# Ordered, gated loads and 256-token pieces in layer 1 of the first batch of a windowed-attention and MLP kernel

## The chip, the cores and the metric
The kernel runs on one NeuronCore of a Trainium2 chip. The metric is the device time of one execution in microseconds (us); lower is better.

## What is computed
Attention over four batches of 768 tokens, 8 heads of 64, in which a query sees the first 4 tokens and the 128 tokens up to its own, and then a two-layer MLP with a squared ReLU on the concatenated heads:

```
scores = q @ k.T / 8          # (4, 8, 768, 768), fp32 inputs
keep   = (key < 4) | (0 <= query - key < 128)
a      = softmax(where(keep, scores, -1e9))
x      = (a @ v) as (3072, 512)
out    = square(relu(x @ w_in)) @ w_out     # w_in (512, 2048), w_out (2048, 512)
```

## The kernel before
All work is written as small operations (`op`, L47) with the engines that may run them, what they come after, and which buffers they take. `Plan.run` (L50) walks through them once, while the program is built, and fixes for each engine an order of instructions; on the chip each engine runs its own list in order and waits on semaphores. So a planned time moves an instruction in a list, and only the list reaches the chip.

A batch goes through these steps. q and k are loaded in fp32 into `qr` and v into `vf` (`load_qk`, L267, `load_v`, L283, both on SP's queue), two heads to a load. `regroup` casts q and k to bf16 (`qs`), PE transposes them into PSUM (`pt`, L342), `unload` copies them to `qkT_sb`. `cast` brings v to bf16 (`v_sb`). `sink_scores` (`pk`) and `scores` (`ps`, L421) multiply, ScalarE takes the exponentials (`es`, `expm`, L435), `domask` multiplies a mask in on VectorE or cuts triangles on GpSimd, `values` (`po`, L470) multiplies with v, `norm` divides by the row sum, `bridge` (`px`, L498) transposes again, and `bridge_copy` writes `xT`. These run in steps s of 256 tokens; s = 0 and 1 are the first 512 tokens, s = 2 the rest. Batch 0 is loaded in two groups, `GROUPS[0]`: 512 tokens and 256; other batches in one.

Layer 1 (`layer1`, L510) multiplies xT with `w_in_sb` into `pm` (L521), ScalarE applies the ReLU (`r`, three buffers), VectorE squares into `gT_sb`. Its pieces are 2 blocks of 128 features by 512 tokens, then 4 blocks by 256 tokens for the last 256. Layer 2 (`layer2`, L536) multiplies `gT_sb` with `w_out_sb` into `py` (L554); the result is copied to `osb` (two buffers) and stored by SP. All PSUM tiles share four banks of 4 KB a partition. Attention of batch b+1 is planned among the two layers of batch b.

The weights come by GpSimd's queue with a cast to bf16: w_in in two halves of 1024 features (`load_w_in`), w_out in four pieces of 512 rows (`load_w_out`). Half 0 of w_in is made to wait for a v load of batch 0; half 1 and w_out wait for nothing of the kind. A DMA on SP also waits, in the built program, for the eighth DMA before it on that queue.

Of the kernel before, what the change touches and what calls it, by code (L numbers as in the profile page):

```python
# [16 lines left out]
LATENCY = 0.2  # L17
# [11 lines left out]
class Op:  # L29
    def __init__(self, key, engines, run, after, takes, reads, dma):  # L30
        self.key, self.engines, self.run = key, engines, run
        self.after, self.takes, self.reads, self.dma = list(after), list(takes), list(reads), dma
        self.end = None


class Plan:
# [4 lines left out]

    def __init__(self, capacity):
        self.ops, self.capacity = [], dict(capacity)

    def op(self, key, engines, run, after=(), takes=(), reads=(), dma=0.0):
        o = Op(key, engines, run, after, takes, reads, dma)
        self.ops.append(o)  # L47
        return o

    def run(self):  # L50
# [4 lines left out]
        blockers = {id(o): len(o.after) for o in waiting}  # L55
        users = {}
        for o in waiting:
            for a in o.after:
                users.setdefault(id(a), []).append(o)
# [4 lines left out]
        while left:  # L64
            best = None
            for o in ready:
# [10 lines left out]
                if not ok:  # L77
                    continue
                pick = None
# [21 lines left out]
            o.end = end  # L101
# [5 lines left out]
            for u in users.get(id(o), ()):  # L107
                blockers[id(u)] -= 1
                if not blockers[id(u)]:
                    u.at = max(a.end for a in u.after) + LATENCY  # L110
# [5 lines left out]
def kernel(  # L116
# [28 lines left out]
    sizes = dict(bank=4, qr=10, qs=6, vf=4, expm=8, r=3, osb=2)  # L145
# [16 lines left out]
    vs_in = consts.tile([32, B, D + 1], BF16)  # L162
# [28 lines left out]
    def build_ident(e):  # L191
        nc.vector.memset(ident, 1.0)
        nc.gpsimd.affine_select(out=ident, in_=ident, compare_op=ALU.is_equal, fill=0.0,
                                base=0, pattern=[[-1, 128]], channel_multiplier=1)

# [7 lines left out]
    def build_masks(e):  # L203
        nc.vector.memset(tri, 1.0)
        for i in range(2):
            triangles(tri[:, i:i + 1, :], i, 1)
        for h2 in range(2):
# [5 lines left out]
    def build_sink_constants(e):  # L213
        nc.vector.memset(head_rows, 1.0)
        nc.vector.memset(vs_in[:, :, D:D + 1], 1.0)
        for i in range(2):
            nc.vector.memset(kblk[i], 0.0)
            nc.vector.memset(vs_sb[i], 0.0)
            nc.vector.memset(v_sb[i][:, :, :, D:D + 1], 1.0)
# [7 lines left out]

    c_ident = op(-9, {"pool": 0.5}, build_ident)
    c_masks = op(-0.95, {"pool": 1.5}, build_masks)
    c_sinks = op(-0.94, {"pool": 1.0}, build_sink_constants)  # L230
    c_vs = op(-0.93, {"pool": 0.3},
              lambda e: nc.gpsimd.dma_start(out=vs_in[:, :, 0:D],
                                            in_=v[:, :, 0:NSINK, :].rearrange("b h s d -> (h s) b d"))
              if False else [nc.gpsimd.dma_start(out=vs_in[:, b, 0:D], in_=v[b, :, 0:NSINK, :])
                             for b in range(B)],
              after=[c_sinks], dma=0.2)
# [5 lines left out]
    def load_w_in(half, behind):  # L242
        def run(e):
            c = slice(half * (DFF // 2), (half + 1) * (DFF // 2))
            d = nc.gpsimd.dma_start(out=w_in_sb[:, :, c],
                                    in_=moe_w_in[:, c].rearrange("(a p) f -> p a f", p=128))
            if behind is not None:
                after_dma(d, loaded[behind])
            loaded["w_in", half] = d
        w_in_op[half] = op(-0.9 + 0.01 * half, {"pool": 0.6}, run, dma=5.5,  # L250
                           after=[ops[behind]] if behind is not None else ())

    def load_w_out(i):
        def run(e):
            nc.gpsimd.dma_start(
                out=w_out_sb[:, 4 * i:4 * i + 4, :],
                in_=moe_w_out[512 * i:512 * i + 512, :].rearrange("(f p) m -> p f m", p=128))
        w_out_op[i] = op(-0.8 + 0.01 * i, {"pool": 0.6}, run, dma=3.1)
# [7 lines left out]
    GROUPS[0] = [(0, 4), (512, 2)]  # L266

    def load_qk(key, b, m, ti, g, behind=None):
        t0, n = GROUPS[b][g]
        sl = qr_slot[b, m, ti, g] = Slot("qr", 1)  # L270

        def run(e):
            t = qr_t[b, m, ti, g] = work["qr"].tile([128, 2, n * D], FP32, name="qr", tag="qr")
            d = nc.sync.dma_start(  # L274
                out=t,
                in_=(q, k)[ti][b, 2 * m:2 * m + 2, t0:t0 + 128 * n, :].rearrange(
                    "h (p t) d -> p h (t d)", t=n))
            if behind is not None:
                after_dma(d, loaded[behind])
            loaded["qk", b, m, ti, g] = d  # L280
        ops["qk", b, m, ti, g] = op(key, {"sp": 0.1}, run, takes=[sl], dma=16 * (0.012 + n * 256 / 27200.0),
                                    after=[ops[behind]] if behind is not None else ())

    def load_v(key, b, m, g, behind=None):
        t0, n = GROUPS[b][g]
        sl = vf_slot[b, m, g] = Slot("vf", 1)

        def run(e):
            t = vf_t[b, m, g] = work["vf"].tile([128, 2, n, D], FP32, name="vf", tag="vf")
            for h2 in range(2):  # L290
# [380 lines left out]
```

## Time and profile before

| | us |
|---|---|
| median of 3 runs | 265.12 (264.98 to 265.88) |
| the profiled execution | 264.97 |
| its span, first to last instruction | 263.2 |
| PE busy in the span | 223.0 (85%) |
| ScalarE, VectorE, GpSimd busy | 136.2, 118.9, 33.1 |
| first matmul of layer 1, batch 0 | 42.98 |
| first matmul of layer 1, batch 1 | 109.83 |

The rows further down come from this one execution. A matmul's end is modelled and successive matmuls overlap, so a cost per matmul is read from a run of them in the chain of work (a run's time over its count), not from the mean duration. Idle time in brackets names what ended it.

### The profile page before, as it was taken

The numbers are of one execution on the slowest core, as the hardware profiler recorded it, in microseconds if no ns is written. First come the engines' busy times: TensorE is split into PE (matmuls) and PEld (weight loads), VectorE is DVE, ScalarE is ACT, GpSimd is POOL, SyncE is SP. The second block draws the span as 40 slices with busy tenths as digits, with TensorE's granted clock in tenths as the row PEclk, the third lists the DMA queues.
The fourth block names the chain that finished last, engine by engine and source line by source line (L and its number), as shares of the span: only waits on it lengthen the run. The fifth ranks groups of instructions, "written<-read, shape, count | busy, mean of one in ns | idle before, by whom it ended". The sixth has DMA issues, their size and how long they took to land.

```text
span 263.2 us, 4650 instructions
## 1 busy us (share of the span) xinstructions
PE 223.0 (85%) x1913; PEld 133.1 (51%) x1940; DVE 118.9 (45%) x273; ACT 136.2 (52%) x156; POOL 33.1 (13%) x49
## 2 busy tenths in 40 slices
PE   0711068999999988999999999999999999999983
PEld 0510055457565446745755456457654564484431
DVE  6520384689421048955654246457551544331010
ACT  1733014688954098876972455568525455561020
POOL 5710301106000003820000013000000110000000
PEclk9965559999999997999999999999999999999998
DMA  6999998899999952000000120200000312000041
GB/s 197 244 195 196 251 234 234 281 217 307 325 238 349 226 190 82 2 0 2 1 2 0 48 114 4 80 0 2 0 4 0 121 40 82 0 0 2 0 176 63
DMA packets 42885, 29.68 MB, mean 113 GB/s; under 512 B 26480, under 2 KB 38768, under 8 KB 42864
## 3 DMA queue, kind: packets, MB, share of 16 engines
q1 hardware_dynamic: 39376, 25.17, 34.0%
q0 software_dynamic: 3488, 4.21, 9.2%
q8 instruction: 15, 0.25, 0.4%
q14 instruction: 6, 0.05, 0.1%
HBM read 27.30 MB, written 6.29 MB: 128 GB/s over the span
## 4 chain that ended last, share of the span: by engine, by line
PE 73%; SPq 9%; DVE 6%; ACT 6%; DMA 3%; issue 2%; DVEq 0%; ACTq 0%
PE py L554 31%; PE pm L521 29%; SPq L291 7%; PE po L470 5%; DMA qr<-in_q_dram 3%; PE ps L421 3%; ACT r L529 2%; PE pt L342 2%; PE px L498 2%; ACT expm L435 2%; SPq L274 2%; DVE xn_sb L484 1%; PE pk L391 1%; DVE expm L444 1%; DVE gT_sb L534 1%
## 5 line engine op out<-in xcount | busy, mean ns | idle before, releaser
L554 PE MATMUL py<-w_out_sb,gT_sb 128*128 128x512 bf16 x367 | 86.5, 379 | 2.5 <-DVE osb L179 0.8
L521 PE MATMUL pm<-xT,w_in_sb 128*128 128x256 bf16 (+1 forms) x504 | 86.1, 325 | 1.4 <-ACT xT L177 0.9
L521 PEld LDWEIGHTS <-w_in_sb 128*128 128x128 bf16 x512 | 49.6, 98 | 33.8 <-issue 1.7
L529 ACT ACTIVATE r<-pm 128x1024 bf16<-128x1024 f32 x48 | 49.1, 1025 | 29.1 <-PE pm L521 24.7
L554 PEld LDWEIGHTS <-gT_sb 128*128 128x128 bf16 x384 | 35.9, 98 | 41.9 <-issue 3.8
L435 ACT ACTIVATE expm<-ps 128x1024 bf16<-128x1024 f32 (+1 forms) x48 | 42.9, 953 | 19.6 <-PE ps L421 19.3
L534 DVE TENSOR_TENSOR gT_sb<-r 128x1024 bf16<-128x1024 bf16 x48 | 33.2, 691 | 43.6 <-ACT r L529 43.6
L444 DVE TENSOR_TENSOR expm<-expm,mask 128x1024 bf16<-128x1024 bf16 (+1 forms) x41 | 26.4, 657 | 32.8 <-ACT expm L435 32.1
L342 PE MATMUL pt<-ident,qs 128*128 128x128 bf16 x192 | 15.2, 236 | 20.0 <-POOL qs L181 12.5
L198 POOL TENSOR_SCALAR_AFFINE_SELECT expm<-expm 128x512 bf16<-128x512 bf16 x14 | 8.6, 635 | 133.1 <-ACT expm L435 133.1
L177 ACT ACTIVATE osb<-py 128x1024 f32<-128x1024 f32 (+1 forms) x9 | 8.4, 952 | 31.3 <-PE py L554 13.6
L342 PEld LDWEIGHTS <-qs 128*128 128x128 bf16 x192 | 12.9, 105 | 22.7 <-POOL qs L181 12.9
L421 PE MATMUL ps<-qkT_sb 64*128 64x128 bf16 (+1 forms) x256 | 16.0, 252 | 8.2 <-DVE qkT_sb L179 5.6
L470 PEld LDWEIGHTS <-expm 128*128 128x128 bf16 x352 | 18.6, 103 | 4.6 <-issue 1.5
L470 PE MATMUL po<-v,expm 128*128 128x65 bf16 x352 | 19.8, 202 | 1.0 <-ACT expm L435 0.6
L177 ACT ACTIVATE qkT_sb<-pt 128x768 bf16<-128x768 bf16 (+1 forms) x18 | 13.4, 768 | 9.8 <-PE pt L342 5.5
L484 DVE TENSOR_TENSOR xn_sb<-po,rc 128x256 bf16<-128x256 f32 x48 | 18.1, 419 | 0.0
L179 DVE COPY qkT_sb<-pt 128x768 bf16<-128x768 bf16 (+2 forms) x22 | 15.2, 710 | 6.3 <-PE pt L342 4.0
L421 PEld LDWEIGHTS <-qkT_sb 64*128 64x128 bf16 x256 | 9.3, 99 | 15.9 <-issue 13.8
L177 ACT ACTIVATE xT<-px 128x1024 bf16<-128x1024 bf16 x8 | 8.2, 1024 | 17.0 <-PE px L498 16.9
L179 DVE COPY osb<-py 128x1024 f32<-128x1024 f32 (+2 forms) x5 | 4.8, 956 | 23.9 <-PE py L554 19.3
L470 PE MATMUL po<-vs,es 128*128 128x65 bf16 x128 | 14.3, 199 | 0.0
(38 smaller groups left out, 104.9 us busy)
## 6 DMA issues: line engine op xcount, KB each, us to landing
out_dram<-osb SPq DMA_DIRECT2D x11, 512.0 KB, 2.9
qr<-in_k_dram SPq DMA_DIRECT2D x12, 384.0 KB, 6.7
qr<-in_q_dram SPq DMA_DIRECT2D x12, 384.0 KB, 6.6
vf<-in_v_dram SPq DMA_DIRECT2D x24, 192.0 KB, 4.4
w_in_sb<-in_moe_w_in_dram POOLq DMA_DIRECT2D x2, 1024.0 KB, 12.0
w_out_sb<-in_moe_w_out_dram POOLq DMA_DIRECT2D x4, 512.0 KB, 13.6
qr<-in_k_dram SPq DMA_DIRECT2D x4, 256.0 KB, 4.5
qr<-in_q_dram SPq DMA_DIRECT2D x4, 256.0 KB, 4.9
```

What stands on the lines that cost most here:

```text
L177: nc.scalar.activation(out=dst, in_=src, func=AF.Copy)
L179: nc.vector.tensor_copy(out=dst, in_=src)
L342: nc.tensor.matmul(pt[:, ti, 128 * t:128 * t + 128], lhsT=qs[:, t, :, :], rhs=ident, is_transpose=True, start=(t == 0), stop=(t == n - 1))
L421: nc.tensor.matmul(ps[:, h2, o:o + w], lhsT=qkT_sb[r, m, 1, 128 * c:128 * c + 128], rhs=qkT_sb[r, m, 0, 128 * qb:128 * qb + w], start=(i = ...
L435: nc.scalar.activation(out=x[:, :, o:512], in_=bank_t["s", b, s, m][:, :, o:512], func=AF.Exp, scale=scale)
L444: nc.vector.tensor_mul(x[:, :, o:512], x[:, :, o:512], mk[:, :, o:512])
L470: nc.tensor.matmul(pv[:, i, h2, :], lhsT=lhsT, rhs=rhs, start=(n_ == 0), stop=(n_ == len(mms) - 1))
L484: nc.vector.tensor_tensor(out=xn_sb[:, 2 * s + i, 128 * m0:128 * m0 + 256].rearrange("p (j h d) -> p j h d", j=2, d=D), in0=pv[:, i, :, :, ...
L521: nc.tensor.matmul(pm[:, i, :], lhsT=w_in_sb[:, kb, 128 * fb:128 * fb + 128], rhs=xT[:, kb, c0:c0 + cw], start=(kb == 0), stop=(kb == NKB ...
L529: nc.scalar.activation(out=r, in_=bank_t.pop(tag), func=AF.Relu)
L534: (nc.vector if e == "dve" else nc.gpsimd).tensor_mul(gT_sb[:, fbs[0]:fbs[0] + n, c0:c0 + cw], r, r)
L554: nc.tensor.matmul(pm[:, i, :], lhsT=gT_sb[:, fb, 128 * t:128 * t + 128], rhs=w_out_sb[:, fb, :], start=(fb == 0), stop=(fb == NFB - 1))
```

## The change
- All loads of a queue are written in one stated order (`dma_op`), and a chain keeps the plan from reordering them. SP: q, k of batch 0's first 512 tokens; v of these; the four sink loads; q, k, v of its last 256; then batches 1, 2 and 3.
- Loads are larger: q and k go four heads at a time (the first two pairs by two heads), v by tiles of 128 tokens and all 8 heads.
- Gates: w_in half 0 behind the second v tile; batch 0's last 256 tokens behind w_in half 0; w_out behind the first v tile of these; batch 1 behind the third piece of w_out.
- `qr` has 5 buffers of four heads instead of 10 of two, `vf` 3 of 256 tokens. `cast` goes by steps of 256 tokens.
- Batch 0's layer 1 runs its first 512 tokens as 4 blocks by 256 tokens, in the order (half 0, s 0), (half 0, s 1), (half 1, s 0), (half 1, s 1) by their keys; what PE's list makes of it has the first piece of half 1 in third place.
- Constants: all fills go to VectorE first; masks are copied behind them; the sink rows (`vs_in`) become fp32 and move from GpSimd's queue to SP's.
- The plan counts the eight DMAs that a queue may have outstanding.

```diff
-    sizes = dict(bank=4, qr=10, qs=6, vf=4, expm=8, r=3, osb=2)
+    sizes = dict(bank=4, qr=5, qs=6, vf=3, expm=8, r=3, osb=2)
...
+                if o.dma:
+                    past = landed.get(next(iter(o.engines)), ())
+                    if len(past) >= 8:
+                        t = max(t, past[-8])
...
+    def dma_op(queue, name, run, us, behind=None, takes=()):
+
+        def go(e):
+            ds = run(e)
             if behind is not None:
...
+                for d in ds:
+                    after_dma(d, loaded[behind])
+            loaded[name] = ds[-1]
+        o = op(-5, {queue: 0.5 if queue == "sp" else 0.85}, go, dma=us, takes=takes,
+               follow=[chained[queue]] if queue in chained else (),
+               after=[ops[behind]] if behind is not None else ())
+        ops[name] = chained[queue] = o
+        return o
...
+    def load_v(b, s, behind=None):
+
+        sl = vf_slot[b, s] = Slot("vf", 1)
+        for i in range(2):
+            t = 2 * s + i
...
+                return [nc.sync.dma_start(
+                    out=vf_t[b, s][:, i], in_=v[b, :, 128 * t:128 * t + 128, :].rearrange("h p d -> p h d"))]
...
-    for m in range(NP):
+    for m0, nm in ((0, 1), (1, 1), (2, 2)):
         for ti in (1, 0):
-            load_qk(-3 + 0.01 * m, 0, m, ti, first)
-    for m in range(NP):
-        load_v(-2 + 0.01 * m, 0, m, first)
-    load_w_in(0, ("v", 0, 2, first))
-    load_w_in(1, None)
...
+            load_qk(0, m0, nm, ti, first)
+    for s in range(2):
+        load_v(0, s)
+    c_vs = dma_op("sp", "vs_in", lambda e: [
+        nc.sync.dma_start(out=vs_in[:, b, 0:D], in_=v[b, :, 0:NSINK, :]) for b in range(B)], 0.2)
...
+    load_w_in(0, 5.7, ("v", 0, 1))
+    load_w_in(1, 8.7)
+    for m0 in (0, 2):
         for ti in (1, 0):
...
+            load_qk(0, m0, 2, ti, rest, behind=("w_in", 0) if m0 == 0 and ti == 1 else None)
+    load_v(0, 2)
     for i in range(4):
-        load_w_out(i)
+        load_w_out(i, ("v", 0, 4) if i == 0 else None)
+    BEHIND = {1: ("w_out", 2), 2: None, 3: None}
...
-        for i, fb in enumerate(range(0, NFB, 2)):
-            layer1(b, b + 0.333 * i / 8, (fb, fb + 1), 0, 512, (0, 1))
+        if b == 0:
+            for half in range(2):
+                for s in range(2):
+                    for i in range(2):
+                        fb = 8 * half + 4 * i
+                        layer1(b, 0.167 * half + 0.083 * s + 0.042 * i, range(fb, fb + 4), 256 * s, 256, (s,))
+        else:
+            for i, fb in enumerate(range(0, NFB, 2)):
+                layer1(b, b + 0.333 * i / 8, (fb, fb + 1), 0, 512, (0, 1))
```

SP's queue at the start, before (two heads to a load; `128x2x256` is 128 partitions of 2 heads by 256 numbers, four tokens each):

```order
L274 DMA qr<-in_k_dram 128x2x256
L274 DMA qr<-in_q_dram 128x2x256
L291 DMA vf<-in_v_dram 128x4x64 x8
L274 DMA qr<-in_k_dram 128x2x128
L274 DMA qr<-in_q_dram 128x2x128
```

The same queue after, whole from its third load to batch 1's first v:

```order
L301 DMA qr<-in_k_dram 128x2x256
L301 DMA qr<-in_q_dram 128x2x256
L301 DMA qr<-in_k_dram 128x4x256
L301 DMA qr<-in_q_dram 128x4x256
L318 DMA vf<-in_v_dram 128x8x64 x4
L625 DMA vs_in<-in_v_dram 32x1x64 x4
L301 DMA qr<-in_k_dram 128x4x128
L301 DMA qr<-in_q_dram 128x4x128
L301 DMA qr<-in_k_dram 128x4x128
L301 DMA qr<-in_q_dram 128x4x128
L318 DMA vf<-in_v_dram 128x8x64 x2
L301 DMA qr<-in_k_dram 128x4x384
```

Eight loads of q and k became six, eight of v four; before, batch 1's first loads stood among batch 0's last ones, now they stand behind all of these.

GpSimd's queue at the start, before:

```order
L221 AFFINE_SELECT head_rows<-head_rows 32x8
L224 AFFINE_SELECT head_rows<-head_rows 32x8
L245 DMA w_in_sb<-in_moe_w_in_dram 128x4x1024
L234 DMA vs_in<-in_v_dram 32x1x64 x4
L255 DMA w_out_sb<-in_moe_w_out_dram 128x4x512 x4
L181 CAST v_99<-vf 128x2x4x64
L245 DMA w_in_sb<-in_moe_w_in_dram 128x4x1024
```

And after:

```order
L233 AFFINE_SELECT head_rows<-head_rows 32x8
L236 AFFINE_SELECT head_rows<-head_rows 32x8
L270 DMA w_in_sb<-in_moe_w_in_dram 128x4x1024 x2
L201 AFFINE_SELECT expm<-expm 128x4x128 x4
L189 CAST qs<-qr 128x256 x5
L277 DMA w_out_sb<-in_moe_w_out_dram 128x4x512 x4
L201 AFFINE_SELECT expm<-expm 128x4x128 x2
```

Both halves of w_in now stand ahead of w_out, and behind the waiting w_in and w_out issues stand triangle cuts and casts of batch 0.

ScalarE around the first layer-1 results of batch 1 (`r`; `v_100` is here batch 3's v), before:

```order
L435 ACTIVATE expm<-ps 128x1024 x2
L177 ACTIVATE xT_103<-px 128x4x256
L177 ACTIVATE qkT_sb<-pt 128x768 x4
L177 ACTIVATE v_100<-vf 128x12x64
L529 ACTIVATE r<-pm 128x1024 x7
```

And after:

```order
L457 ACTIVATE expm<-ps 128x1024 x8
L185 ACTIVATE xT_103<-px 128x4x256
L185 ACTIVATE qkT_sb<-pt 128x768 x3
L185 ACTIVATE v_100<-vf 128x2x8x64
L551 ACTIVATE r<-pm 128x1024 x2
```

The cast of batch 3's v stands ahead of batch 1's layer-1 results in both.

## Rows read from the trace of the kernel before

**Rows 1.** The page's 40 slices of 6.58 us, tenths: PE, granted clock, DMA.
```profile
PE   0711068999999988999999999999999999999983
...
PEclk9965559999999997999999999999999999999998
DMA  6999998899999952000000120200000312000041
```

**Rows 2.** Busy us of engines by stage, then granted clock, DMA share, GB/s.
```profile
0.00:42.98 42.98, 13.49 (x172) 10.62 (x173) 20.73 (x66) 14.02 (x19) 12.60 (x23) 0.72 1.07 227
42.98:109.83 66.85, 62.42 (x598) 39.02 (x605) 34.28 (x78) 45.66 (x54) 11.15 (x13) 0.97 0.84 225
109.83:263.20 153.37, 147.03 (x1145) 83.49 (x1162) 63.89 (x131) 76.50 (x83) 9.32 (x14) 0.99 0.08 32
```

**Rows 3.** Timeline of the start: start, us, engine, line, operation, [idle before <-releaser].
```profile
4.33 0.93 POOL L245 DMA_DIRECT2D w_in_sb<-in_moe_w_in_dram  x1
...
4.87 19.14 SPq L291 DMA_DIRECT2D vf<-in_v_dram  x8
...
8.93 2.33 POOL L255 DMA_DIRECT2D w_out_sb<-in_moe_w_out_dram  x3
...
30.39 0.43 DVE L179 CAST v<-vf 128x512 bf16<-128x512 f32 x1 [10.34 <-DMA vf<-in_v_dram]
...
30.83 0.74 POOL L245 DMA_DIRECT2D w_in_sb<-in_moe_w_in_dram  x1 [5.39 <-DMA vf<-in_v_dram]
...
40.86 2.07 ACT L177 ACTIVATE xT<-px 128x1024 bf16<-128x1024 bf16 x2 [3.06 <-PE px L498]
...
42.98 2.32 PE L521 MATMUL pm<-xT,w_in_sb 128*128 128x512 bf16 x9 [0.89 <-ACT xT L177]
```

**Rows 4.** The tile w_in_sb: from issue to landing of its two loads.
```profile
DMA to landing us min/median/max: 11.7/12.0/12.4
```

**Rows 5.** Four stretches of 4 us, columns as in rows 2; GB/s stands last.
```profile
0.00:4.00 4.00, 0.00 (x0) 0.00 (x0) 2.23 (x15) 1.28 (x1) 1.07 (x8) 1.00 0.49 147
4.00:8.00 4.00, 1.70 (x16) 1.63 (x16) 3.00 (x10) 0.60 (x1) 3.93 (x6) 1.00 0.94 283
...
64.00:68.00 4.00, 3.21 (x32) 2.04 (x31) 3.96 (x11) 2.84 (x5) 1.11 (x1) 1.00 1.03 366
...
88.00:92.00 4.00, 4.00 (x20) 1.80 (x19) 0.00 (x0) 0.00 (x0) 0.00 (x0) 1.00 1.16 209
```

**Rows 6.** The page's DMA queue of the weights: packets, MB, share of 16 engines.
```profile
q0 software_dynamic: 3488, 4.21, 9.2%
```

**Rows 7.** The tile vf: from issue to landing of the v loads.
```profile
DMA to landing us min/median/max: 1.9/5.5/16.7
```

**Rows 8.** Groups by shape: the long exponentials; busy us, mean ns, idle before.
```profile
L435 ACT ACTIVATE expm<-ps 128x1024 bf16<-128x1024 f32 x32 | 31.1, 1023 | 15.5 <-PE ps L421 15.3
```

**Rows 9.** The chain of work in order of time: start, us, engine, tile, count.
```profile
37.07 2.58 PE po L470 x48
...
75.90 1.75 PE pm L521 x16
77.64 0.86 PE py L554 x4
...
155.99 0.55 PE ps L421 x12
...
157.51 0.74 PE po L470 x24
...
159.11 0.45 PE px L498 x8
159.56 0.67 PE pt L342 x12
```

**Rows 10.** Timeline of SP's queue, and of ScalarE later: batch 3's v.
```profile
81.62 9.27 SPq L291 DMA_DIRECT2D vf<-in_v_dram  x8
...
111.82 0.84 ACT L177 ACTIVATE v<-vf 128x768 bf16<-128x768 f32 x1
```

More of the change, by code (lines that the diff above doesn't have):

```diff
@@ L29, with __init__ @@
 class Op:
-    def __init__(self, key, engines, run, after, takes, reads, dma):
+    def __init__(self, key, engines, run, after, takes, reads, dma, follow):
         self.key, self.engines, self.run = key, engines, run
         self.after, self.takes, self.reads, self.dma = list(after), list(takes), list(reads), dma
-        self.end = None
+        self.follow = list(follow)
+        self.end = self.issued = None
 class Plan:
@@ L43, in __init__, with op @@
         self.ops, self.capacity = [], dict(capacity)
-    def op(self, key, engines, run, after=(), takes=(), reads=(), dma=0.0):
-        o = Op(key, engines, run, after, takes, reads, dma)
+    def op(self, key, engines, run, after=(), takes=(), reads=(), dma=0.0, follow=()):
+        o = Op(key, engines, run, after, takes, reads, dma, follow)
         self.ops.append(o)
@@ L54, in run @@
         waiting = list(self.ops)
-        blockers = {id(o): len(o.after) for o in waiting}
+        blockers = {id(o): len(o.after) + len(o.follow) for o in waiting}
+        landed = {}
         users = {}
         for o in waiting:
-            for a in o.after:
+            for a in o.after + o.follow:
                 users.setdefault(id(a), []).append(o)
@@ L100, in run @@
                 end = queue + DMA_LATENCY
-            o.end = end
+                landed.setdefault(e, []).append(end)
+            o.end, o.issued = end, start + cost
             for s in o.reads:
@@ L109, in run @@
                 if not blockers[id(u)]:
-                    u.at = max(a.end for a in u.after) + LATENCY
+                    u.at = max([a.end + LATENCY for a in u.after] + [a.issued for a in u.follow])
                     ready.append(u)
@@ L226, in build_sink_constants @@
                                 base=NSINK - 1, pattern=[[NSINK, H]], channel_multiplier=-1)
[L228 to L236, printed above, removed]
+    c_fill = op(-9, {"dve": 2.5}, fill)
@@ L239 @@
+    c_ident = op(-9, {"pool": 0.3}, build_ident)
+    c_tri = op(-0.9, {"pool": 0.6}, build_triangles)
+    c_masks = op(-0.9, {"dve": 1.5}, build_masks, after=[c_tri])
+    c_sinks = op(-0.8, {"pool": 0.5}, build_head_rows)
     loaded = {}
     w_in_op, w_out_op = {}, {}
[L242 to L246, printed above, removed]
-            if behind is not None:
[L248 to L251, printed above, removed]
@@ new lines, in load_w_in, with load_w_out @@
+    def load_w_in(half, us, behind=None):
+        c = slice(half * (DFF // 2), (half + 1) * (DFF // 2))
+        w_in_op[half] = dma_op(
+            "pool", ("w_in", half),
+            lambda e: [nc.gpsimd.dma_start(out=w_in_sb[:, :, c],
+                                           in_=moe_w_in[:, c].rearrange("(a p) f -> p a f", p=128))],
+            us, behind)
+    def load_w_out(i, behind=None):
+        w_out_op[i] = dma_op(
+            "pool", ("w_out", i),
+            lambda e: [nc.gpsimd.dma_start(
@@ L275, in run @@
                 out=t,
[L276 to L290, printed above, removed]
-                d = nc.sync.dma_start(
-                    out=t[:, h2],
-                    in_=v[b, 2 * m + h2, t0:t0 + 128 * n, :].rearrange("(t p) d -> p t d", p=128))
-                if behind is not None:
-                    after_dma(d, loaded[behind])
-            loaded["v", b, m, g] = d
-        ops["v", b, m, g] = op(key, {"sp": 0.2}, run, takes=[sl], dma=16 * n * 0.0214,
-                               after=[ops[behind]] if behind is not None else ())
@@ L555, in mm @@
                                      rhs=w_out_sb[:, fb, :], start=(fb == 0), stop=(fb == NFB - 1))
[L556 to L557 removed]
+            need = [o for x, o in ops.items() if x[0] == "sq" and x[1] == b
+                    and x[3] <= 128 * t < x[3] + x[4] and 4 * part - 2 < x[2] < 4 * part + 4]
             a = op(keys(i, part), {"pe": 0.865}, mm, after=last + need + [w_out_op[part]],
```

96 lines of the change are left out of this document (52 added, 44 removed).

## The prediction, made before the changed kernel ran
> **What bounds the kernel now.** I read the slices first [rows 1]: TensorE (PE) is nearly idle in the first 40 us and 90% busy or more from there on, its granted clock falls towards half (the 1.2 GHz level) in slices 3 to 6, and the DMA engines are full from slice 1 to slice 14. So there are two regimes. The stage table cuts them [rows 2]: PE does 13.5 us of work in the first 42.98 us, 62.4 in the next 66.85, and 147.0 in the last 153.37. The first cut is the first matmul of batch 0's layer 1, the second that of batch 1's layer 1. The last stage is full; only the first, and the waits of the second, can give anything.
>
> What the first stage waits for stands in its rows [rows 3]. GpSimd issues the second half of w_in at 4.33 us and three pieces of w_out from 8.93, ahead of anything that PE can use them for. The v loads of batch 0 go out at 4.87, and the queue takes 19.14 us to push eight of them out. VectorE gets its third v piece at 30.39 after 10.34 us of idleness, and only then is w_in's first half issued (30.83, behind a 5.39 us wait). It lands 11.7 to 12.4 us after its issue [rows 4], which is 42.5 to 43.2: in the same microsecond in which the last xT copy ends (42.93) and PE starts (42.98). Two chains end there together, loads and attention, and both were fed late by the same cause: weights that were not yet wanted took the DMA engines.
>
> **What the DMA engines can do.** Read sizes follow from the shapes: q and k of batch 0's first 512 tokens 2.1 MB, its v 1.05 MB, the last 256 tokens half of that, q and k of any other batch 3.15 MB and v 1.57 MB. Rates come from stretches with one kind in flight: 366 GB/s for q and k rows (64 to 68 us), 209 for 256-byte v rows (88 to 92), and 283 for the first q and k (4 to 8) [rows 5]. The weight queue took 9.2% of 16 engines' span, 24.2 us, for 4.21 MB written [rows 6]: 6.05 us for a half of w_in, 3.03 for a piece of w_out. No row shows a weight load alone; it lies between these 6.05 and the 12.4 us of [rows 4], which were measured with other loads in flight. I take 6.05, since the engines do little else behind the gate.
>
> **The change, part by part.**
> (1) Loads in order. q and k of the first 512 tokens run without weights beside them: 0.59 MB by 4 us (147 GB/s over them [rows 5]), the rest at 283 to 366 GB/s, done at 8 to 9.3; I take 9. v then needs 5.0 us, to 14.0, and its second piece is done at 11.5. The gate of w_in half 0 opens there plus a receipt (a v load of 64 KB takes at least 1.9 us from issue to landing [rows 7], so up to some 1.5), 12.5, and issuing costs 0.93 [rows 3]: 13.4. Plus 6.05 it lands at 19.5, with its receipt 20.5; at the slow end, 13.4 + 12.4, at 25.8. Before: 43.
> (2) The attention chain. All of the first v has landed at about 14.5. ScalarE is then the long one: a v cast of about 1.0 (0.84 for three quarters of its columns [rows 10]), then five exponentials (three of 1.02 [rows 8], two a quarter shorter), the small sink one and an xT copy of about 1.03 (two took 2.07) [rows 3]: some 7.0 us without a wait, 21.5. In the profile the same chain took 12.5 us from the last v (30.39) to the last xT [rows 3], with batch 0's last q and k pushed in between, and at half clock; that end gives 27. With 256-token pieces layer 1 needs only the first xT, so I take 22.5 for layer 1's start, a microsecond above the bare chain, ends 20.5 and 27. This is 20.5 us earlier than before.
> (3) 256-token pieces of layer 1. They turn 64 matmuls of 512 columns into 128 of 256. 16 of 256 take 1.75 us and four of 512 (of layer 2) 0.86 [rows 9], so the columns cost the same: 128 x 0.109 = 14.0 against 64 x 0.215 = 13.8. ScalarE's and VectorE's pieces stay 128x1024. Taken at nothing (ends 0 and +0.5).
> (4) A new wait. In PE's new order the third piece belongs to w_in half 1, and PE comes to it about 4 us after its start, at 26.5. Half 1 follows half 0 in the queue: 25.5 alone, up to 28.4 if it shares with the 1.05 MB of q and k that the landing of half 0 releases (2.9 us). Receipt included, 29 is my value: 2.5 us of wait, ends 0 and 5.
> (5) The later gates. q, k, v of batch 0's last third, 5.4 us, share with w_in half 1 and end near 32; w_out's four pieces take 12.1, to 45 to 47, the first landed at some 37, and PE first wants w_out at about 40. Batch 1's loads start behind the third piece and take 8.6 + 7.5, to 61 to 63; their first pair is there at about 51, and PE comes to it at about 55. These margins are three or four microseconds, so the loads hide when the prices hold, and I book 0 with an end of +5. A landing that gates the next load leaves engines empty only where no other queue has work: at w_out's first piece, some 1.5 us.
> (6) Constants. ident, tri and the zero fills go to VectorE first; they are the same instructions in another order, ahead of the same first casts, and the first cast moves to ScalarE. Nothing, ends 0 and 0.5. The four small sink loads move from GpSimd's queue to SP's, behind the v loads: hidden, since SP's next load waits for w_in anyway.
> (7) Fewer buffers (qr 5 of twice the size, vf 3). SP's output stores now stand between batch 3's loads; batch 0's third output copy waits for the first store. That lies ahead of PE's need by my times; 0, end +2.
>
> **The sum.** Between the two cuts PE streams, per [rows 9], 192 matmuls of 256 columns (21.0 us), 96 of 512 (20.6), 88 transposes at 0.67 per 12 (4.9), 88 scores at 0.55 per 12 (4.0), 168 value products at 0.74 per 24 (5.2), 32 of the bridge at 0.45 per 8 (1.8) and the sink scores, four of 512 columns and four of 256 (1.3): 58.8. Before, the stage took 66.85, so 8.0 were waits. After: 2.5 for w_in half 1; about 1.5 for the clock, since PE is sparse from 10 to 22 us as it was before (0.5 granted in those slices [rows 1]; 48 value products took 2.58 us there against 0.74 for 24 at full clock [rows 9], 1.1 us lost); and 3.5 for the stretch where batch 1's attention is no longer covered by layer 2 (half of what the old stage lost). Layer 1 of batch 1 starts at 22.5 + 58.8 + 7.5 = 88.8 instead of 109.83. The remaining 153.37 us have the same matmuls in nearly the same order, with PE 96% busy as it is, so they stay. The span shrinks by 21.0. The profiled execution took 264.97, 1.77 more than its span and 0.15 under the median of the three runs: 264.97 - 21.0 = 243.9 us.
>
> **The rivals.**
> (A) The load stream becomes the floor. ScalarE and VectorE cast batch 3's v just ahead of batch 1's first layer-1 results in the new order; before, batch 3's v was also cast about there (111.82), but its last load had been issued by 90.9, 21 us earlier [rows 10]. Summed from (1) and (5), batch 3's v lands near 95. VectorE's squares wait behind the cast, PE can run three r buffers and three to four banks ahead, some 9 us, so a landing at 95 holds back nothing if PE is at 89. If each of the four gates (w_in, batch 0's last third, w_out, batch 1) leaves the engines empty for a least landing, 1.9 us [rows 7], the stream is 7.6 us longer (103) and PE's stage starts in effect at 94 to 97: 249 to 252. For it: those gates, and weight prices that no row shows alone. Against: before, the same bytes were through by about 93, and at three of the gates another queue has work left. The Trainium skill, "DMA: Bandwidth & Descriptors", section "Anatomy of one DMA — SWDGE (gpsimd) path", puts a fixed cost of about 2 us on a load, most of it the wait for the receipt; paid at each of the four gates it would be 8 us and this rival, where the sum books one gate of 1.5. The 1.9 us agree with the figure, but no row here shows a gate with nothing else in flight. Chance 0.22.
> (B) Attention, not weights, starts layer 1: if the chain takes its old 12.5 us from v on, 27 instead of 22.5, the time is 248 to 249. It lies in my range; 0.08.
> (C) Slower: weights alone are slow. If GpSimd's queue moves a half of w_in in 12.4 us even when it has the engines to itself, half 0 lands at 25.8 and half 1 at 38, w_out ends at 63, batch 1's loads at 77, batch 3's v near 111: the stage starts near 102, 257 us. It turns into a loss when the four halves (w_out counts as two) cost another 8 us, from about 14.4 us a half; at 16 the stage starts at 116 and the time is some 271 us. No row reached that. 0.07, of which 0.04 end slower than before and 0.01 within 0.3% of it.
> (D) All gaps close better than booked (no wait for half 1, no clock loss, layer 1 at 21): 21 + 58.8 + 3.5 = 83.3, held by (A)'s mechanism to about 85.5: 240.6. 0.13.
> The forecast, 242 to 247: 0.50.
>
> **How the numbers follow.** 0.3% (0.8 us) is about what a measurement of this kernel can tell from no change. The range 239.0 to 251.5 holds the forecast, D, B and most of A; what is left out is C, the upper part of A and a little of D, 0.2. Faster 0.95, same 0.01, slower 0.04.
>
> **What would show it.** Right: first layer-1 matmul at 21 to 25 us, a PE wait for w_in a few us later, full clock from about 30 on, layer 1 of batch 1 at 86 to 92, and about 153 us from there to the end. A late w_in half 0 (landing over 12 us after issue) speaks for C; ScalarE's or VectorE's v casts of batches 2 and 3 waiting on DMA, with PE waiting for their copies, for A; xT later than w_in for B. Wrong altogether if the last stage grows, or if PE waits for q and k of batch 1.

## The result, and the profile of the changed kernel

| | before | changed |
|---|---|---|
| median of 4 runs each, us | 265.32 | 251.04 (250.02 to 252.04) |
| ratio, 95% interval | | 0.946 (0.942 to 0.950) |
| the profiled execution | 264.97 | 250.02 |
| its span | 263.2 | 248.3 |
| first matmul of layer 1, batch 0 | 42.98 | 24.54 |
| first matmul of layer 1, batch 1 | 109.83 | 94.23 |
| from there to the end | 153.37 | 154.07 |

The time fell by 14.3 us, into the stated range (239.0 to 251.5) near its upper end. It is 7.1 us above the point of 243.9.

The page's 40 slices, now of 6.21 us, answer [rows 1]: TensorE, its granted clock, the DMA engines, in tenths.

```profile
PE   1467999999997679999999999999999999999983
...
PEclk9997999999999799999999999999999999999998
DMA  5989969998999999100001302000002220000051
```

The start in which TensorE is under eight tenths has shrunk from six slices to four, and the clock is at its lower level (1.2 GHz) for only part of one slice there. But slices 12 to 14 (counted from 0) have a new dent, with the clock down in one of them, shortly before the loads end in slice 15. The table of stretches answers [rows 2]; busy us of PE, PEld, DVE, ACT, POOL, then granted clock, DMA share, GB/s.

```profile
0.00:24.54 24.54, 12.63 (x156) 9.40 (x157) 16.98 (x53) 14.16 (x19) 5.79 (x15) 0.93 0.91 201
24.54:78.50 53.96, 52.89 (x492) 36.78 (x498) 31.51 (x60) 30.95 (x38) 9.68 (x14) 1.00 1.04 246
78.50:94.23 15.73, 10.22 (x176) 8.13 (x174) 8.86 (x24) 11.83 (x13) 7.04 (x9) 0.89 1.05 309
94.23:248.30 154.07, 147.85 (x1156) 84.24 (x1176) 63.82 (x130) 77.21 (x83) 9.15 (x13) 0.99 0.12 43
```

From 24.54 on TensorE is full for 54 us (1.1 us idle); then, in the last 15.7 us before batch 1's layer 1, it is idle for 5.5 and partly at the low clock. The timeline of the start answers [rows 3]: start, us, engine, line, operation, idle before and its releaser.

```profile
13.61 1.66 POOL L270 DMA_DIRECT2D w_in_sb<-in_moe_w_in_dram  x2 [11.26 <-DMA vf<-in_v_dram]
...
21.91 0.38 SPq L301 DMA_DIRECT2D qr<-in_k_dram  x1
...
23.47 1.02 ACT L185 ACTIVATE xT<-px 128x1024 bf16<-128x1024 bf16 x1 [2.03 <-PE px L520]
...
24.54 1.91 PE L543 MATMUL pm<-xT,w_in_sb 128*128 128x256 bf16 x16 [0.26 <-ACT xT L185]
...
26.73 5.40 PE L543 MATMUL pm<-xT,w_in_sb 128*128 128x256 bf16 x48
```

SP's load at 21.91 is gated by w_in's first half, so that half had landed by then, 8.3 us after its issue. The xT copy ends 2.6 us later and starts layer 1: attention, not the weights, is last. The row of 48 matmuls runs through three pieces without a stop, the first on half 1 among them, so there is no wait for half 1.

The dent is told by the chain that ended last, from 72.66 to 94.23 (start, us, what):

```profile
72.66 6.30 DMA vf<-in_v_dram
...
79.05 1.08 ACT v L185
...
80.84 10.60 DMA out_dram<-osb
...
91.47 1.23 DVE osb L187
92.69 0.60 DVE expm L466
...
94.23 0.39 PE pm L543
```

And by the timeline of the engines on it:

```profile
64.22 13.50 SPq L318 DMA_DIRECT2D vf<-in_v_dram  x6
...
65.13 1.02 ACT L185 ACTIVATE osb<-py 128x1024 f32<-128x1024 f32 x1
...
79.05 1.07 ACT L185 ACTIVATE v<-vf 128x1024 bf16<-128x1024 f32 x1 [4.59 <-DMA vf<-in_v_dram]
...
79.95 0.84 SPq L301 DMA_DIRECT2D qr<-in_q_dram  x1
80.02 3.74 ACT L457 ACTIVATE expm<-ps 128x1024 bf16<-128x1024 f32 x4
80.84 0.97 SPq L593 DMA_DIRECT2D out_dram<-osb  x1
...
81.06 0.40 PE L443 MATMUL ps<-qkT_sb 64*128 64x128 bf16 x6 [1.88 <-ACT expm L457]
...
91.47 1.23 DVE L187 COPY osb<-py 128x1024 f32<-128x1024 f32 x1 [2.92 <-DMA out_dram<-osb]
```

Two waits stand in series. ScalarE's list has a cast of batch 2's v, which only batch 2's attention needs, ahead of four exponentials of batch 1; it stands 4.59 us at the head of the queue until v lands. And the store of batch 0's first output tile is issued at 80.84, behind q and k of batch 3 on the same queue. It lands 10.6 us later, where a store takes 2.8 in the median. VectorE's copy of the third tile waits for that store, because `osb` has two buffers; the mask that batch 1's attention needs stands behind the copy. The 10.6 us are only the second part of that store's delay: its tile was ready at 66.15, but SP's list has the six v loads of batch 2, which take 13.50 us to push, and batch 3's four q and k loads ahead of it, so it is issued 14.7 us later.

### The profile page after: what moved, and what is told of

Its sections match the earlier page's. It is cut to its first block, busy times and chain, and to the rows that moved or that the text cites. A ratio compares the mean times of both kernels' runs of the same rounds, so it can differ in the third digit from the quotient of the medians.

```text
span 248.3 us, 4710 instructions
## 1 busy us (share of the span) xinstructions
PE 223.6 (90%) x1978; PEld 138.6 (56%) x2004; DVE 121.2 (49%) x265; ACT 134.2 (54%) x153; POOL 31.7 (13%) x51
## 3 DMA queue, kind: packets, MB, share of 16 engines
q0 software_dynamic: 3168, 4.19, 10.1%
## 4 chain that ended last, share of the span: by engine, by line
PE 65%; DMA 17%; ACT 7%; DVE 4%; SPq 3%; issue 2%; ACTq 0%; DVEq 0%
PE pm L543 28%; PE py L576 25%; DMA vf<-in_v_dram 7%; DMA qr<-in_k_dram 6%; DMA out_dram<-osb 4%; PE po L492 4%; PE ps L443 3%; ACT r L551 3%; PE pt L364 3%; SPq L301 2%; PE px L520 2%; ACT expm L457 2%; DVE osb L187 1%; ACT v L185 1%; DVE gT_sb L556 1%
## 5 line engine op out<-in xcount | busy, mean ns | idle before, releaser
L543 PEld LDWEIGHTS <-w_in_sb 128*128 128x128 bf16 x576 | 55.6, 98 | 28.4 <-issue 1.6
L556 DVE TENSOR_TENSOR gT_sb<-r 128x1024 bf16<-128x1024 bf16 x48 | 35.3, 738 | 30.0 <-ACT r L551 30.0
L466 DVE TENSOR_TENSOR expm<-expm,mask 128x1024 bf16<-128x1024 bf16 (+1 forms) x38 | 24.4, 649 | 23.9 <-ACT expm L457 23.4
L201 POOL TENSOR_SCALAR_AFFINE_SELECT expm<-expm 128x512 bf16<-128x512 bf16 x20 | 12.8, 663 | 100.5 <-ACT expm L457 100.5
L185 ACT ACTIVATE osb<-py 128x1024 f32<-128x1024 f32 (+1 forms) x8 | 7.4, 943 | 21.8 <-PE py L576 13.7
L187 DVE COPY osb<-py 128x1024 f32<-128x1024 f32 (+2 forms) x6 | 6.0, 1001 | 26.8 <-PE py L576 19.3
L364 PEld LDWEIGHTS <-qs 128*128 128x128 bf16 x192 | 13.0, 104 | 10.2 <-ACT qs L185 4.3
L185 ACT ACTIVATE qkT_sb<-pt 128x768 bf16<-128x768 bf16 (+2 forms) x20 | 14.2, 723 | 8.2 <-DVE qkT_sb L187 5.8
L187 DVE COPY qkT_sb<-pt 128x768 bf16<-128x768 bf16 (+2 forms) x20 | 14.5, 740 | 6.3 <-PE pt L364 4.4
L443 PEld LDWEIGHTS <-qkT_sb 64*128 64x128 bf16 x256 | 9.6, 100 | 13.4 <-issue 11.1
L185 ACT ACTIVATE qs<-qr 128x768 bf16<-128x768 f32 (+2 forms) x10 | 7.4, 736 | 15.2 <-DMA qr<-in_k_dram 14.4
## 6 DMA issues: line engine op xcount, KB each, us to landing
w_in_sb<-in_moe_w_in_dram POOLq DMA_DIRECT2D x2, 1024.0 KB, 10.9
```

What stands on the lines that cost most here:

```text
L185: nc.scalar.activation(out=dst, in_=src, func=AF.Copy)
L187: nc.vector.tensor_copy(out=dst, in_=src)
L364: nc.tensor.matmul(pt[:, ti, 128 * t:128 * t + 128], lhsT=qs[:, t, :, :], rhs=ident, is_transpose=True, start=(t == 0), stop=(t == n - 1))
L443: nc.tensor.matmul(ps[:, h2, o:o + w], lhsT=qkT_sb[r, m, 1, 128 * c:128 * c + 128], rhs=qkT_sb[r, m, 0, 128 * qb:128 * qb + w], start=(i = ...
L466: nc.vector.tensor_mul(x[:, :, o:512], x[:, :, o:512], mk[:, :, o:512])
L543: nc.tensor.matmul(pm[:, i, :], lhsT=w_in_sb[:, kb, 128 * fb:128 * fb + 128], rhs=xT[:, kb, c0:c0 + cw], start=(kb == 0), stop=(kb == NKB ...
```

## The experiments

All kernels are variants of the changed kernel; times are medians against the kernel before on the same chip (265.8 to 265.9 in all of them). Three theories on the dent: **Q**, finished work is held behind late loads in queues that run in order, by two waits in series; **R**, ScalarE is the bound of that stretch; **S**, the stream of loads is the floor.

| run | us | ratio, 95% interval |
|---|---|---|
| e1 late cast | 252.91 | 0.951 (0.946 to 0.955) |
| e2 three output buffers | 247.83 | 0.933 (0.929 to 0.937) |
| e3 both | 242.53 | 0.913 (0.909 to 0.917) |
| e4 no gates | 267.31 | 1.004 (1.001 to 1.007) |
| e5 e3 with 512-token blocks | 245.55 | 0.925 (0.920 to 0.929) |
| e6 e3 with the weight gates alone | 254.74 | 0.959 (0.955 to 0.962) |
| e7 e3 with `qr` 6 | 242.24 | 0.911 (0.906 to 0.916) |
| e8 e3 with the old constants | 240.20 | 0.904 (0.900 to 0.908) |
| e9 old fills and masks alone | 242.62 | 0.914 (0.910 to 0.918) |
| e10 old sink loads alone | 244.76 | 0.921 (0.917 to 0.925) |
| e11 e8 with `qr` 6 | 245.72 | 0.924 (0.919 to 0.930) |
| e12 e3's order, two output buffers | 256.34 | 0.963 (0.958 to 0.969) |

**e1**, the cast made to wait for batch 1's attention:
```diff
-                                       after=[ops["v", b, 2 * s], ops["v", b, 2 * s + 1], c_sinks] + older_values,
+                                       after=[ops["v", b, 2 * s], ops["v", b, 2 * s + 1], c_sinks] + older_values
+                                       + ([ops["values", b - 1, NS - 1, 2]] if b >= 2 else []),
```


> One edit to the changed kernel: the casts of v of batches 2 and 3 may run only after the last value product of the batch before, so that no cast of a late load stands ahead of batch 1's exponentials. Theory Q (finished work is held behind late loads in in-order queues, at two places in a row: ScalarE's cast of batch 2's v, 4.6 us of waiting at 79.05, and VectorE's third output copy, which waits until 91.4 for a store that stands behind 3.15 MB of batch 3's q and k): the first wait goes, the second still holds VectorE until about 91, so the time stays within 1 us of 251.0. Rival R (the stretch is bound by ScalarE's eight exponentials and their chain, the waits are filled time): also within 1 us, with the copy no longer late. Rival S (the load stream as such is the floor): no change, and layer 1 of batch 1 starts at 93 to 95 as now.

252.91 us, 1.9 above the changed kernel and not to be told from it: the intervals overlap. ScalarE's wait for v is gone, but the store now holds ScalarE instead (timeline):

```profile
80.00 12.68 SPq L594 DMA_DIRECT2D out_dram<-osb  x3
...
91.26 1.02 ACT L185 ACTIVATE osb<-py 128x1024 f32<-128x1024 f32 x1 [6.70 <-DMA out_dram<-osb]
...
92.33 2.29 PE L544 MATMUL pm<-xT,w_in_sb 128*128 128x512 bf16 x5 [6.83 <-ACT osb L185]
```

**e2**, a third output buffer:
```diff
-    sizes = dict(bank=4, qr=5, qs=6, vf=3, expm=8, r=3, osb=2)
+    sizes = dict(bank=4, qr=5, qs=6, vf=3, expm=8, r=3, osb=3)
```


> One edit to the changed kernel: three osb buffers instead of two, so batch 0's third output copy waits for no store. Theory Q: the 2.9 us for which VectorE waited for the store go, ScalarE's wait for batch 2's v stays: layer 1 of batch 1 starts at 91 to 92, 247.5 to 249.0 us. Rival R: under 1 us, 250 to 251. Rival S: layer 1 of batch 1 starts earlier but PE then waits for squares behind the cast of batch 3's v, which lands at 98.7 in any case: 250 to 251.

247.83 us. No engine waits for a store any more; the cast still waits:

```profile
78.27 1.07 ACT L185 ACTIVATE v<-vf 128x1024 bf16<-128x1024 f32 x1 [4.21 <-DMA vf<-in_v_dram]
```

**e3**, both edits together:

> Both edits together. Theory Q: both waits go and they follow one another on one chain, so more than the sum of the two alone: layer 1 of batch 1 starts at 87 to 89, 244 to 246 us. Rival R: 249.5 to 251. Rival S: 249 to 251, with PE waiting for loads of batch 2 or 3 elsewhere.

242.53 us, 8.5 less than the changed kernel and 1.5 below the least that I gave it; the two alone gave +1.9 and -3.2: the sign of two waits in series. Its stretches (columns as above) and the start of batch 1's layer 1:

```profile
24.60:87.84 63.24, 60.73 (x652) 43.19 (x649) 37.81 (x78) 40.16 (x49) 15.03 (x23) 1.00 1.00 249
87.84:242.50 154.66, 149.62 (x1203) 84.92 (x1200) 66.44 (x135) 80.69 (x88) 10.46 (x15) 1.00 0.17 58
```

The same bytes with the same prices, and the stretch is 6.5 us shorter: S falls as the bound of 251. ScalarE is busy for 40.2 of 63.2 us and does the same operations: R falls too. The profiled execution of this run was its slowest (244.22), so some of its stretches are shorter in the median.

**e12**, the wait for the store alone. e1 to e3 differ also in the order that the planner writes, so a last kernel keeps e3's order on every engine and takes only the third buffer away at run time:
```diff
-    work = {n: ctx.enter_context(tc.tile_pool(name=n, bufs=c)) for n, c in sizes.items() if n != "bank"}
+    work = {n: ctx.enter_context(tc.tile_pool(name=n, bufs=2 if n == "osb" else c)) for n, c in sizes.items() if n != "bank"}
```


> The kernel with both edits (242.5 us), in exactly its order of instructions on every engine, but with two output buffers instead of three at run time; the planner still plans with three. Nothing else differs, so this prices the wait for the store alone, free of what another order brings. Theory Q: batch 0's third output copy, which ran at 81.7 with three buffers, must again wait for the store of the first tile, which stands behind batch 3's loads and lands at about 91; VectorE or ScalarE holds it at the head of its queue, the masks and casts behind it wait too, and layer 1 of batch 1 starts at 92 to 95 instead of 87.8: 247 to 252 us. Rival N: the third buffer helped mainly because the planner then found a better order; in the same order its lack costs little, 242.5 to 244.5 us.

256.34 us, 13.8 more than e3 and worse than either theory had. The chain, then the timeline:

```profile
82.07 11.62 DMA out_dram<-osb
```
```profile
93.78 1.23 DVE L187 COPY osb<-py 128x1024 f32<-128x1024 f32 x1 [14.17 <-DMA out_dram<-osb]
...
95.66 0.29 PE L493 MATMUL po<-v,expm 128*128 128x65 bf16 x2 [11.51 <-DVE expm L467]
...
100.95 3.62 PE L544 MATMUL pm<-xT,w_in_sb 128*128 128x512 bf16 x15
```

VectorE stands 14.2 us at a copy that nobody needs soon, TensorE 11.5 behind the mask after it, and layer 1 starts 13.1 us later than in e3. This is Q with everything else equal. In the changed kernel the same copy comes later in VectorE's list, so its wait is only 2.92 us; how its dent splits between cast and store can't be read off a single number, and no run takes the wait of the cast alone away with the order held fixed.

**e4**, the gates off, order and sizes kept (`behind` dropped from w_in half 0, batch 0's last q and k, w_out, and batch 1):

> The changed kernel with its large loads, its stated order on each queue, its 256-token pieces and constants, but none of the four gates: each queue issues as soon as its order and its buffers allow. Theory G (the gates are what brings layer 1 forward, since weights otherwise take the engines from q, k and v): the last v of the first 512 tokens lands after 25 us, layer 1 starts at 33 to 40 us, 258 to 264 us. Rival (few large loads in order do it, gates add nothing): layer 1 at 24 to 27, 249 to 253 us.

267.31 us: the whole gain is gone, 3.3 us more than theory G's upper end, and layer 1 starts 5 us later than it had. The weights go out at 1.41 and 3.05, and v waits for them (timeline):

```profile
1.41 1.67 POOL L270 DMA_DIRECT2D w_in_sb<-in_moe_w_in_dram  x2
...
4.66 26.47 SPq L318 DMA_DIRECT2D vf<-in_v_dram  x4
...
34.68 0.69 DVE L187 CAST v<-vf 128x1024 bf16<-128x1024 f32 x1 [7.76 <-DMA vf<-in_v_dram]
...
45.16 1.91 PE L543 MATMUL pm<-xT,w_in_sb 128*128 128x256 bf16 x16 [0.20 <-ACT qkT_sb L185]
```

So fewer and larger loads in a stated order are worth nothing by themselves; with the gates they are. The planner also writes quite another order here, but v's late landing stands in the trace. No run puts gates on the small loads of before, so whether the gates would do it alone is open.

**e6**, e3 with the gates on the weights alone:
```diff
-            load_qk(0, m0, 2, ti, rest, behind=("w_in", 0) if m0 == 0 and ti == 1 else None)
+            load_qk(0, m0, 2, ti, rest)
...
-    BEHIND = {1: ("w_out", 2), 2: None, 3: None}
+    BEHIND = {1: None, 2: None, 3: None}
```


> The kernel with both edits (242.5 us), with only the gates on the weights left (w_in's first half behind batch 0's second v, w_out behind w_in's second half); the last third of batch 0's q and k is no longer held behind w_in's first half, nor batch 1's loads behind w_out. Theory: the gates work because what is needed first gets the DMA engines alone; without these two, SP's loads run as far ahead as their buffers allow and share the engines with w_in. The first half, which landed about 21.9, then comes 3 to 6 us later and is last instead of xT at 24.5: 244 to 249 us. Rival: the buffers of q, k and v hold SP's loads back by themselves, the gates on SP's loads are worth nothing, and the time stays within 1 us of 242.5.

254.74 us, above what I gave it, and by another way. (The expectation names w_out's gate wrongly: the edit leaves w_out behind batch 0's fifth v tile, and that tile is no longer held back itself.) Half 0 of w_in was hardly slower (8.9 us from issue to landing). But the planner, with no gate to reckon with, puts the transposes of batch 0's last k and q into TensorE's list ahead of layer 1; these share the DMA engines with the weights, and TensorE stands in front of the first of them (timeline). Layer 1 starts at 36.6.

```profile
26.71 0.39 PE L364 MATMUL pt<-ident,qs 128*128 128x128 bf16 x2 [8.58 <-POOL qs L189]
```

**e5**, e3 with batch 0's layer 1 in 512-token blocks:
```diff
-        if b == 0:
-            for half in range(2):
-                for s in range(2):
-                    for i in range(2):
-                        fb = 8 * half + 4 * i
-                        layer1(b, 0.167 * half + 0.083 * s + 0.042 * i, range(fb, fb + 4), 256 * s, 256, (s,))
-        else:
-            for i, fb in enumerate(range(0, NFB, 2)):
-                layer1(b, b + 0.333 * i / 8, (fb, fb + 1), 0, 512, (0, 1))
+        for i, fb in enumerate(range(0, NFB, 2)):
+            layer1(b, b + 0.333 * i / 8, (fb, fb + 1), 0, 512, (0, 1))
```


> The kernel with both edits (late cast of v, three output buffers; 242.5 us), but batch 0's layer 1 again in blocks of 512 tokens, as before the change. Theory: layer 1 can then start only when both xT tiles of the first 512 tokens exist. With both edits the first xT copy ended at 24.50 and the second at 28.35, so TensorE starts layer 1 at about 28.4 instead of 24.6 and stands idle for most of the 3.8 us, less the score and transpose work it can put there: 245 to 246.5 us. Rival: the 3.8 us are only moved into gaps that exist later (there are 3.1 us of TensorE idle between 24.6 and 87.8), and the time stays at 242 to 243 us: the 256-token pieces would then be worth nothing.

245.55 us, 3.0 more: the pieces are worth about the wait for the second xT, as far as a re-sorted order lets it be told. TensorE's first matmul of layer 1 (timeline):

```profile
27.42 0.58 PE L544 MATMUL pm<-xT,w_in_sb 128*128 128x512 bf16 x1 [1.11 <-ACT xT L185]
```

**e7**, `qr=5` to `qr=6` in e3; every engine's order stays word for word the same:

> The kernel with both edits (242.5 us), with six buffers for raw q and k instead of five, so that SP's sixth load (at 4.15 us, behind the first cast of k that ended at 4.12) needs no buffer back. Theory: the v loads behind it are issued about 0.8 us earlier (4.56 became 3.8), so w_in's first half, which goes out behind v, is issued and landed 0.5 to 0.8 us earlier; but the first xT is last (24.5 against about 21.9), and the q and k it needs share the engines with v all the same: no change, 242 to 243 us. Rival: the attention chain of the first 512 tokens waits for that sixth load's q (landed about 11.1), and layer 1 starts 0.8 us earlier: 241.7 us.

242.24 against 242.53 us, within the scatter. Layer 1 starts 0.6 us earlier (24.00), which the theory denied, but at the end it can't be told.

**e8 to e11**, the constants; the expectations of e9 to e11 weigh two theories, C (casts that come late hold v back, and the first q and k gain) and V (the sinks' v goes early). e8 puts back both halves of their move: the fills and masks in three operations, and the sinks' v through GpSimd's queue as bf16. e9 puts back only the fills and masks, e10 only the sinks' v, e11 is e8 with `qr=6`. The edit of the sinks:
```diff
-    c_vs = dma_op("sp", "vs_in", lambda e: [
-        nc.sync.dma_start(out=vs_in[:, b, 0:D], in_=v[b, :, 0:NSINK, :]) for b in range(B)], 0.2)
+    c_vs = dma_op("pool", "vs_in", lambda e: [
+        nc.gpsimd.dma_start(out=vs_in[:, b, 0:D], in_=v[b, :, 0:NSINK, :]) for b in range(B)], 0.2)
```


> The kernel with both edits (242.5 us), with the constants built as before the change: the memsets in three operations on GpSimd's slots, the sinks' v loaded through GpSimd's queue as bf16. Theory: nothing waits for a constant in the start (the first mask is used at 12.4, the sinks' rows later), so moving them is worth 0 to 1 us: 242 to 243.5 us. Rival: GpSimd's queue, with 3.7 us more of issues and some fills ahead of w_in, sends w_in later by as much, and layer 1 starts that much later: 245 us or more.

> The kernel with both edits (242.5 us), with the constants built in the three operations of before the change, but the sinks' v still loaded through SP's queue as float32 (the other half of the constants' move is kept). With both halves undone the time fell to 240.2 us and layer 1 began at 22.97 instead of 24.57. Theory C (casts late, so v late): VectorE does the masks and memsets first and casts q and k only at 5.75, SP's sixth load waits for that cast and is sent at 6.26 instead of 4.15, v at 6.67 instead of 4.56, and the first 512 tokens' q and k have the DMA engines longer to themselves (the fifth load landed 8.6 instead of 9.4). Then this run keeps the gain: 240 to 241 us, layer 1 at 23 to 23.8. Rival V (the sinks' v): the gain came from the sinks' v being sent at 4.3 through GpSimd's queue instead of at 11.9 through SP's, ahead of the sinks' product on VectorE; then this run stays at 242.5 us.

> The kernel with both edits (242.5 us), with only the sinks' v moved back to GpSimd's queue as bf16; the constants are built where the change builds them. Theory C (late casts hold v back) gives no gain: 242 to 243 us. Rival V (the sinks' v early, and four issues less on SP's queue) gives 240 to 241 us.

> The kernel with both edits and the constants as before the change (240.2 us), with six buffers for raw q and k: SP's sixth load and the v behind it are then sent at about 3.3 and 3.9 without waiting for the late cast. Theory C: this takes away what held v back, the fifth load lands at 9.2 to 9.4 again instead of 8.6, and layer 1 begins 0.6 to 1.6 us later: 241 to 242 us. Rival V, or that only the order of instructions after the planner counted: 240 us or a little less, since nothing else waits.

e8 is the fastest kernel of the study (240.20 us), 2.3 under e3. But e9 (242.62) shows nothing of it, e10 (244.76) is slower, and e11 (245.72) loses 5.5 against e8. C and V both fall. C's first step is there: in e8 and e9 v goes out at 6.67, and the fifth load's k is cast at 8.61 and 8.32 instead of 9.44. Yet layer 1 of e9 starts at 24.12, only 0.45 us before e3's. Beside the constants the kernels differ in the order that the planner writes. In e9 it is nearly e3's (TensorE's, GpSimd's and SP's lists are the same), and so is the time; in e8, e10 and e11 every engine's list differs from e3's. Two stretches of TensorE, in e8 and in e11 (columns as above), show where it tells:

```profile
64.00:70.00 6.00, 5.95 (x58) 3.74 (x59) 4.56 (x11) 5.96 (x9) 3.46 (x3) 1.00 1.06 373
```
```profile
64.00:70.00 6.00, 3.89 (x29) 2.22 (x28) 5.14 (x9) 3.67 (x5) 1.56 (x2) 0.93 1.05 374
```

In e11 the sink scores of batch 1 wait for exponentials there, in e8 they don't. That the order makes the difference is what these runs leave as the explanation; it isn't shown, since no run re-sorts the lists and changes nothing else. The times lie from 2.3 below e3 to 3.2 above it. e1 to e6 carry the same doubt of a few us; e7 and e12, with e3's order unchanged, don't.

## Why the prediction was right, and where its steps failed

The span was forecast at 263.2 - 21.0 = 242.2 and came out at 248.3, 6.1 more: 2.0 in the start, 3.4 in the stretch between the layer-1 starts, 0.7 behind it.

- **(1) Loads in order: right, a little short.** w_in half 0 had landed by 21.9 instead of 20.5, from an issue at 13.6 instead of 13.4: 8.3 us for a half that I priced at 7.1 with its receipt. The lower price from the queue's share [rows 6] was the nearer end; the 12.4 of [rows 4] was a load with others beside it. Part of the 8.3 is a stretch behind the gate in which next to nothing moves; see (5).
- **(2) The attention chain: right in kind, 2.0 short.** Layer 1 starts at 24.54, not 22.5, and xT is last, as rival B had it (for 27). The sum hung the start on v's landing, at 14.5. The chain that ended last hangs on a k load instead:

```profile
2.82 6.84 DMA qr<-in_k_dram
```

  So the term that was too small is the first loads: this k landed at 9.67 and the last q was cast at 11.31, where I had both landed at 9, and what stands behind them on the path (casts, transposes, scores) is in no term of the sum. The stretches 4 to 8 and 8 to 12 moved 255 and 262 GB/s, the second with v rows in it, where I had 283 to 366. The 12.5 us of the upper end were counted from the third of the four v casts (30.39); the fourth began at 31.56.
- **(3) 256-token pieces at nothing: right** on price (the row of 48 takes 5.40 us, 0.113 each, where I had 0.109); as the key to starting with one xT they are worth some 3 us (e5).
- **(4) A wait for w_in half 1 of 2.5 us: wrong,** it is zero. Half 1 was there by 28.0, a microsecond before my 29, and TensorE, which started 2.0 us later, came to it after that.
- **(5) The later gates hide: right. One gate leaves the engines empty for 1.5 us: too little.** Two do, w_in's and w_out's (stretches of 1 us, DMA share and GB/s last; then GpSimd's timeline):

```profile
14.00:15.00 1.00, 0.71 (x8) 0.58 (x6) 0.95 (x3) 0.54 (x2) 1.00 (x2) 1.00 0.28 58
15.00:16.00 1.00, 0.34 (x4) 0.20 (x4) 1.00 (x2) 0.85 (x3) 1.00 (x3) 1.00 0.99 41
...
32.00:33.00 1.00, 1.00 (x16) 0.94 (x14) 0.78 (x3) 0.82 (x1) 0.68 (x2) 1.00 0.18 34
33.00:34.00 1.00, 1.00 (x12) 0.90 (x10) 1.00 (x3) 0.68 (x3) 1.00 (x3) 1.00 0.01 1
34.00:35.00 1.00, 1.00 (x16) 0.94 (x14) 0.49 (x3) 1.00 (x2) 1.00 (x2) 1.00 0.21 32
```
```profile
32.32 0.75 POOL L189 CAST qs<-qr 128x256 bf16<-128x256 f32 x2 [1.21 <-PE pt L364]
33.01 2.99 POOL L277 DMA_DIRECT2D w_out_sb<-in_moe_w_out_dram  x4
```

  At w_in's gate 58 and 41 GB/s move where 207 to 211 do from 17 on: by these rates an estimated 1.5 us, part of w_in's 8.3, which cost nothing since xT was last. At w_out's it is 2.6 us, with TensorE busy all through; w_out is issued straight behind two casts on GpSimd, so not all of that is the gate's. At the other two gates the engines are full (shares of 1.07 to 1.16 from 20 to 25, 0.88 to 1.24 from 44 to 48). The Trainium skill ("DMA: Bandwidth & Descriptors", "Anatomy of one DMA — SWDGE (gpsimd) path") names a fixed cost of about 2 us per load. The two gaps are of that size, but they come at two gates, not at all four as rival A would have had it.
- **(6) Constants at nothing:** within what can be told apart (e8 to e11).
- **(7) Fewer buffers, "0, end +2": the step that failed.** I saw the stores among batch 3's loads and the third copy waiting for the first store, and then wrote "That lies ahead of PE's need by my times". What I didn't price is the store. SP's list holds its issue back by 14.7 us, until the loads ahead of it are pushed. Then batch 3's q and k, 3.15 MB, are ahead of it on the queue; at the stretch's 309 GB/s they need 10.2 us, and the store landed after 10.6. Behind the copy stands a mask on VectorE, behind that TensorE. With the order held fixed this wait is worth 13.8 us (e12); beside the cast, in the changed kernel's own order, it is part of the 5.5 us of idleness and the low clock of the dent.
- **Rival A, in part.** It priced a cast of batch 3's v with VectorE's squares behind it, and named batch 2's casts only among its signs. The cast that cost is batch 2's, on ScalarE, ahead of batch 1's exponentials: the second third of that v was there at 79.0, where my own prices put all of it at 77 to 79, and I hadn't asked who stands behind that cast. Batch 3's last v was cast at 98.70, between the sum's 95 and rival A's 103; the stage behind came out 0.7 longer.

**The sum.** TensorE's own 58.8 us between the two starts is about right: with both waits away (e3) the stretch takes 63.2 us, with TensorE busy for 60.7 of them, that is 4.4 above the 58.8 where I booked 7.5. In the changed kernel it takes 69.7, 10.9 above. The 1.5 booked for the clock don't fall where I had them: the clock is full from 24.54 to 78.50, and low in the start and in the dent. So the forecast of 243.9 was nearly the time of e3 (242.5), a kernel that has two edits more: a start 2.0 us too early and 2.5 us for half 1 that weren't due, against a dent that wasn't booked. The mechanism of the gain, weights held back so that layer 1 starts early, was right, and the rates were near. That the time came within the range is in part luck: rival A had widened it up to there, for another wait than the one that came.

## What to carry to other kernels

When loads are put in one queue in a stated order, list what else stands in that queue, and give each store among them the time until the loads ahead of it are pushed and the bytes ahead of it as its landing time; then look which copy needs that buffer back and what stands behind the copy on its engine. The same holds for a cast that is planned as soon as its load should land: if the load comes late, all that stands behind the cast comes late, and two such waits in series can hide much of one another until both are gone. Gate what isn't needed yet, and give the buffers that drain finished work one more.

## What the runs showed of the hardware

- A store of 512 KB landed in 2.8 us in the median, and in 10.1 to 11.6 when it was issued behind a batch's q and k on the same queue (10.6 in the changed kernel, 11.0 in e3, 10.1 to 11.6 in e8, 11.6 in e12); in e3 nobody waited for it. The Trainium skill ("DMA: Bandwidth & Descriptors", "Queues, rings and completion order") says that a ring's descriptors are taken up in order and that an engine changes between queues at packets. The store that lands behind the loads ahead of it agrees with the first. No run here put the stores on another queue.
- The first half of w_in, with only the second behind it, took 8.3 us from issue to landing in the changed kernel and 8.2 in e3, and 8.9 in e6, where q and k ran beside it. In [rows 4] it was 11.7 to 12.4.
- TensorE's granted clock stayed at the higher level (2.4 GHz) throughout the start in e3 (1.00, TensorE busy for 14.05 us). In the changed kernel it was at half, the lower level, from 18 to 21 us (0.50), a mean of 0.93 over the start, with 12.63 us busy. In the kernel before it had 0.72 over its longer start [rows 2].
